# Both halves of head 0's K on one queue, the first weights held until x has landed, K turned ahead of x, and an earlier filler, at the start of a fused attention kernel

## The chip, the cores and the metric

The kernel runs on one core of one Trainium2 chip. The metric is the device time of one execution in microseconds (us). Every version was run several times and is quoted by its median. Ratios are computed as the mean time of one kernel's runs over the mean time of the other's runs of the same rounds, so they are not quite the ratio of the medians quoted beside them. All runs in this study were of the fast state. They were made in batches on different chips (the record numbers four of them 8, 6, 0 and 14), and each batch timed the kernel before as well, so that versions are compared with the before of their own batch.

Two scales meet here. The whole kernel takes 1939 us. The change moves instructions only in its first 16 us, and what it did is about 1.5 us. That is 0.08%, far inside the band of 2% that counts as "same", so the timings carry little on their own, and the argument is read from the traces of the head.

Times inside a trace are us from the start of the profiled span. One trace is one execution, and executions differ: those of the changed kernel in one batch by up to 2.6 us, those of one of the versions below by 4.0 us.

## The reference, cut to what matters

```python
def reference(A_x, A_k_cache, A_v_cache, A_wq, A_wo, B_x, B_w1, B_w3, B_w2):
    xn = _layernorm(x, axis=-1)              # x: 2048 x 640, bf16
    q  = (xn @ wq) -> 32 heads x 2048 x 192
    scores = q k^T * 192 ** -0.5             # k, v: 32 heads x 2048 x 192
    o  = softmax(scores) v
    s  = o @ wo
    g  = silu((silu(xn @ w1) * (xn @ w3)) @ w2)
    return x + s * g
```

## The kernel before

The kernel streams 1024 blocks of scores through TensorE (matmuls), with one exponential of each block on ScalarE. Before the first exponential can run, a head must be worked through: x's first group of 512 rows lands, is normalised, is turned (transposed by TensorE against an identity matrix, then copied by ScalarE or VectorE out of the tile in PSUM that the turns write), and is multiplied by head 0's weights. Head 0's K must be turned and copied as well. K comes in two halves, K0 and K1; each needs 16 turns of 128x128. The weights W come in three parts, all issued by GpSimd.

```python
def load_w0():                       # three loads on GpSimd's queue
    W = wqp.tile([P, 2 * DC, P], BF16, tag="W", name="W")
    nc.gpsimd.dma_start(out=W[:, 0:DC, :], ...)             # first part, 160 KB
    nc.gpsimd.dma_start(out=W[:, DC:2 * DC, 0:PGW], ...)    # second part, 80 KB
    nc.gpsimd.dma_start(out=W[:, DC:2 * DC, PGW:P], ...)    # third part, 80 KB
    ...

def turn_over(k):                    # filler: keeps TensorE busy until data is there
    for i in range(k):
        nc.tensor.matmul(warm, lhsT=ident_bf[:], rhs=ident_bf[:], start=True, stop=True)

def head_start():
    load_x(0, 0, 2)                  # x's first group, SyncE's queue
    load_x(0, 2, 4)
    load_k0(0, nc.sync)              # K0
    load_w0()
    turn_over(44)
    ln_stats(0, 0)                   # statistics of x: three tiles on VectorE, one on ScalarE
    ln_stats(0, 1)
    ln_stats_act(0, 3)
    load_k0(1, nc.scalar)            # K1, ScalarE's queue
    load_x(1, queue=nc.scalar)       # x's second group
    load_v(0, (0,), nc.scalar)       # first half of head 0's V
    ...                              # rest of the statistics; rstd (1/deviation, by pow) on GpSimd
    load_w(1)                        # weights of head 1, GpSimd's queue
    for i in range(4):
        ln_norm(0, i, nc.vector)     # four normalisations on VectorE
    pk0 = ps_o.tile([P, 4, 512], BF16, tag="ob0", name="pk0")
    ln_turn(0, 0, nc.scalar.copy)            # turn x's first half, copy on ScalarE
    turn_k0(pk0, 0, range(4))                # 16 turns of K0
    ln_turn(0, 1, nc.vector.tensor_copy)     # turn x's second half, copy on VectorE
    turn_k0(pk1, 1, (0, 1))                  # 8 turns of K1
    swap_halves(0)
    copy_k0(nc.scalar.copy, pk0, 0, 0)       # copies of K0's turns
    copy_k0(nc.scalar.copy, pk0, 0, 1)
    copy_k0(nc.vector.tensor_copy, pk1, 1, 0)
    load_v(0, (1,))
    load_x(2)
    project_first()                          # 20 matmuls: two x halves, two W halves, 5 each
    turn_k0(pk1, 1, (2, 3))                  # last 8 turns of K1
    copy_k0(nc.scalar.copy, pk1, 1, 1)
    scores(0)
    ...
```

Of the kernel before, what the change touches and what calls it, by code (L numbers as in the profile page):

```python
# [11 lines left out]
BF16 = mybir.dt.bfloat16  # L12
# [3 lines left out]
P = 128  # L16
# [112 lines left out]
def _kernel_impl(  # L129
# [12 lines left out]
    nc = tc.nc  # L142
# [31 lines left out]
    const = ctx.enter_context(tc.tile_pool(name="const", bufs=1))  # L174
# [3 lines left out]
    ident_bf = const.tile([P, P], BF16, name="ident_bf")  # L178
# [25 lines left out]
    ps_o = att.enter_context(tc.tile_pool(name="ps_o", bufs=1, space=bass.MemoryType.PSUM))  # L204
# [4 lines left out]
    x_sb = x_all[:, 0:NQT * D].rearrange("p (t d) -> p t d", d=D)  # L209
# [3 lines left out]
    def load_x(g, t0=0, t1=4, queue=nc.sync):  # L213
        queue.dma_start(out=x_sb[:, 4 * g + t0:4 * g + t1, :],
                          in_=x2[g * 512:(g + 1) * 512, :].rearrange("(p t) d -> p t d", t=4)[:, t0:t1, :])

    def gate_cols(h):
        wsel = B_w1 if h % 2 == 0 else B_w3
        return wsel[:, (h // 2) * PGW:(h // 2 + 1) * PGW]

    def load_w0():
        W = wqp.tile([P, 2 * DC, P], BF16, tag="W", name="W")
        nc.gpsimd.dma_start(out=W[:, 0:DC, :], in_=A_wq[:, 0:P].rearrange("(c p) d -> p c d", p=P))
        nc.gpsimd.dma_start(out=W[:, DC:2 * DC, 0:PGW], in_=gate_cols(0).rearrange("(c p) f -> p c f", p=P))
        nc.gpsimd.dma_start(out=W[:, DC:2 * DC, PGW:P], in_=A_wq[:, P:DH].rearrange("(c p) d -> p c d", p=P))
        loads.setdefault(0, {}).update(W=W)

    def load_w(h):

        W = wqp.tile([P, 2 * DC, P], BF16, tag="W", name="W")  # L230
        nc.gpsimd.dma_start(out=W[0:64, :, :], in_=A_wq[:, h * DH:h * DH + P].rearrange("(j p) d -> p j d", p=64))
        if h < 2 * NPIG:
            nc.gpsimd.dma_start(out=W[64:P, :, 0:PGW], in_=gate_cols(h).rearrange("(j p) f -> p j f", p=64))
        else:
            nc.gpsimd.memset(W[64:P, :, 0:PGW], 0.0)
        nc.gpsimd.dma_start(out=W[64:P, :, PGW:P],
                            in_=A_wq[:, h * DH + P:(h + 1) * DH].rearrange("(j p) d -> p j d", p=64))
        loads.setdefault(h, {}).update(W=W)
# [21 lines left out]
    def load_k0(half, queue):  # L260
        if half == 0:
            kn = stp.tile([P, NQT, HG * DH], BF16, tag="ostage", name="kn")
            k0["v"] = kn[:].rearrange("p t c -> p (t c)")[:, 0:NKT * DH].rearrange("p (j c) -> p j c", c=2 * DH)
            loads.setdefault(0, {}).update(KW=kvp.tile([P, 5, HK], BF16, tag="KW", name="KW"))
        queue.dma_start(out=k0["v"][:, half * HP:(half + 1) * HP, :].rearrange("p j c -> p (j c)"),
                          in_=A_k_cache[0, 0, half * HK:(half + 1) * HK, :].rearrange("(p t) d -> p (t d)", p=P))

    def turn_k0(dst, half, sel):
        for a in sel:
            for b in range(HP):  # L270
                nc.tensor.transpose(out=dst[:, a, b * P:(b + 1) * P],  # L271
                                    in_=k0["v"][:, half * HP + b, FIRST[a]:FIRST[a] + P], identity=ident_bf[:])

    def copy_k0(copy, src, half, two):
        KW = loads[0]["KW"]
        ks = slice(half * HP * P, (half + 1) * HP * P)
        copy(out=KW[:, 0:2, ks] if two == 0 else KW[:, 2:5:2, ks], in_=src[:, 2 * two:2 * two + 2, :])
# [5 lines left out]
    def load_v(h, halves=(0, 1), queue=nc.sync):  # L283


        vt = vts[h % 2]
        for t in halves:
            if h == 0:
                queue.dma_start(out=vt[:, t * NPAIR:(t + 1) * NPAIR, 0:DH],
                                  in_=A_v_cache[0, h, t * HK:(t + 1) * HK, :].rearrange("(i s) d -> i s d", i=P))  # L290
            else:
                nc.sync.dma_start(out=vt[:, :, 0:DH].rearrange("i (p t) d -> i p t d", t=2)[:, :, t, :],
                                  in_=A_v_cache[0, h].rearrange("(p i t) d -> i p t d", i=P, t=2)[:, :, t, :])
        loads.setdefault(h, {}).update(vt=vt)

    mhalf = const.tile([P, 4], F32, name="mhalf")
    nc.vector.memset(mhalf[:], -0.5)
    for vt in vts:
# [9 lines left out]
    def ln_stats(g, i):  # L308
        if i == 0:
            lnorm[g] = [lnp.tile([P, 4, n], F32, tag=t, name=t)  # L310
                        for t, n in (("mv", nc.vector.BN_AGGR_DIM), ("ve", 1), ("rstd", 1))]
        mv, ve, rstd = lnorm[g]
        stats = lnp.tile([P, nsub, nc.vector.BN_STATS_DIM], F32, tag="stats", name="stats")
        xr = x_sb[:, 4 * g + i, :].rearrange("p (a f) -> p a f", a=nsub)
        for a in range(nsub):
            nc.vector.bn_stats(out=stats[:, a, :], in_=xr[:, a, :])  # L316
        nc.vector.bn_aggr(out=mv[:, i, :], in_=stats[:])  # L317
        if i % 2 == 1:
            nc.vector.tensor_scalar(out=ve[:, i - 1:i + 1, 0], in0=mv[:, i - 1:i + 1, 1], scalar1=eps, scalar2=None,
                                    op0=ALU.add)  # L320
            ln_rstd(g, i)

    def ln_rstd(g, i):
        mv, ve, rstd = lnorm[g]
        if i % 2 == 1:
            two = slice(i - 1, i + 1)
            nc.gpsimd.tensor_tensor(out=rstd[:, two, 0], in0=ve[:, two, 0], in1=mhalf[:, two], op=ALU.pow)
# [3 lines left out]
    def ln_stats_act(g, i):  # L331


        mv, ve, rstd = lnorm[g]
        ss = lnp.tile([P, 1], F32, tag="ss", name="ss")
        xns[g, i] = xnp.tile([P, D], BF16, tag="xn", name="xn")
        xi = x_sb[:, 4 * g + i, :]
        nc.scalar.activation(out=xns[g, i][:], in_=xi, func=ACT.Identity, scale=1.0 / D, accum_out=mv[:, i, 0:1])
        nc.scalar.activation(out=xns[g, i][:], in_=xi, func=ACT.Square, scale=-1.0, bias=mv[:, i, 0:1], accum_out=ss[:])
        lnorm["ss"] = ss  # L340
# [222 lines left out]

    pk1 = ps_o.tile([P, 4, 512], BF16, tag="ob1", name="pk1")
    warm = pk1[:, 0, 0:2 * P].bitcast(F32)

    def turn_over(k):
        for i in range(k):
            nc.tensor.matmul(warm, lhsT=ident_bf[:], rhs=ident_bf[:], start=True, stop=True)

    def head_start():

        load_x(0, 0, 2)
        load_x(0, 2, 4)
        load_k0(0, nc.sync)
        load_w0()
        turn_over(44)
        ln_stats(0, 0)
        ln_stats(0, 1)
        ln_stats_act(0, 3)  # L580
        load_k0(1, nc.scalar)
        load_x(1, queue=nc.scalar)
        load_v(0, (0,), nc.scalar)
        ln_stats(0, 2)
        mv, ve, _ = lnorm[0]
        nc.vector.tensor_scalar(out=ve[:, 2, :], in0=mv[:, 2, 1:2], scalar1=eps, scalar2=None, op0=ALU.add)
        nc.vector.tensor_scalar(out=ve[:, 3, :], in0=lnorm["ss"][:], scalar1=1.0 / D, scalar2=eps,
                                op0=ALU.mult, op1=ALU.add)
        ln_rstd(0, 3)
        load_w(1)  # L590
        for i in range(4):
            ln_norm(0, i, nc.vector)
        pk0 = ps_o.tile([P, 4, 512], BF16, tag="ob0", name="pk0")
        ln_turn(0, 0, nc.scalar.copy)
        turn_k0(pk0, 0, range(4))
        ln_turn(0, 1, nc.vector.tensor_copy)
        turn_k0(pk1, 1, (0, 1))
        swap_halves(0)
        copy_k0(nc.scalar.copy, pk0, 0, 0)
        copy_k0(nc.scalar.copy, pk0, 0, 1)  # L600
        copy_k0(nc.vector.tensor_copy, pk1, 1, 0)
        load_v(0, (1,))
        load_x(2)
        project_first()
        turn_k0(pk1, 1, (2, 3))
        copy_k0(nc.scalar.copy, pk1, 1, 1)
        scores(0)
        shift_first()
        shift_k0()
        scores(1)  # L610
        ln_stats(1, 0)
        ln_stats(1, 1)
        ln_stats(1, 2)
        ln_norm(1, 0, nc.vector)
        ln_norm(1, 1, nc.vector)
        ln_turn_dma(1, 0)
        ln_turn_dma(1, 1)
        for g in range(3, NQB):
            load_x(g)
        ln_stats(1, 3)  # L620

    head_start()

    def finish_block(n):
# [71 lines left out]
    for qb in range(NQB):  # L696
        qs = slice(qb * 512, (qb + 1) * 512)
        for fl in range(FL2 // P):
            ps = pools[(qb * (FL2 // P) + fl) % 2].tile([P, 1024], F32, tag="st2", name="ps_gu")
            for r, w in enumerate((wrest["w1"], wrest["w3"])):  # L700
                for c in range(DC):
                    nc.tensor.matmul(ps[:, r * 512:(r + 1) * 512], lhsT=w[:, c, fl * P:(fl + 1) * P], rhs=xnT[:, c, qs],  # L702
                                     start=(c == 0), stop=(c == DC - 1))
# [20 lines left out]
    for i in range(NQT):  # L724
        ps = pools[i % 2].tile([P, 1024], F32, tag="st2", name="ps_f")
        for fc in range(FC):
            for b, (c0, c1) in enumerate(DP):
                nc.tensor.matmul(ps[:, b * 512:b * 512 + c1 - c0], lhsT=hT[:, fc, i * P:(i + 1) * P],  # L728
                                 rhs=w2_sb[:, fc, c0:c1], start=(fc == 0), stop=(fc == FC - 1))
# [78 lines left out]
```

## Time and profile before

| | before |
|---|---|
| time, median of 3 runs | 1939.36 us |
| profiled span | 1936.7 us |
| first half of x's first group landed | 3.86 us |
| third part of W landed (last of its 16 packets' signals) | 8.12 us |
| first projection matmul | 10.44 us |
| first exponential | 14.38 us |

In the views PE is TensorE (PEld its weight loads), DVE is VectorE, ACT ScalarE, POOL GpSimd and SP SyncE; a q behind the name is the engine's sequencer, which issues loads. The page of the kernel before: its span, the busy times, the granted TensorE clock in 40 slices of the span, and the shares of the chain that ended last.

```profile
span 1936.7 us, 59668 instructions
...
PE 1927.1 (100%) x27273; PEld 1317.2 (68%) x27281; DVE 654.4 (34%) x997; ACT 1181.5 (61%) x1278; POOL 282.1 (15%) x501
...
PEclk9999999999999999999999999999999999999999
...
PE 99%; DVE 0%; DMA 0%; ACT 0%; issue 0%
```

TensorE is the bound of the kernel, at full clock, once the head is over. So a change of the head pays only by bringing the first exponential forward, and costs as much as it delays it.

The timeline of TensorE in the head, before. Columns: start, duration, engine, line, operation and tiles, count, and in brackets the idle time ahead of the group with what ended it.

```profile
2.78 4.32 PE L569 MATMUL pk<-ident_bf 128*128 128x128 bf16 x44 [2.78 <-POOL ident_bf masks.py:199]
7.90 0.81 PE L354 MATMUL pst<-ident_bf,xn 128*128 128x128 bf16 x10 [0.80 <-DVE xn L346]
8.54 1.06 PE L271 MATMUL pk<-ident_bf,kn 128*128 128x128 bf16 x16
9.44 0.72 PE L354 MATMUL pst<-ident_bf,xn 128*128 128x128 bf16 x10
10.00 0.61 PE L271 MATMUL pk<-ident_bf,kn 128*128 128x128 bf16 x8
10.44 2.35 PE L391 MATMUL ps<-xnT,W 128*128 128x256 bf16 x20
```

Read it as a queue, since TensorE ran its matmuls in the order of the program: filler (`pk<-ident_bf`), x's first turns (`pst`), K0's turns (`pk<-ident_bf,kn`), x's second turns, half of K1's, and then the projection (`ps`) in one piece. There is almost no idle time from 7.90 on: K's turns sit in the holes that x leaves.

The timeline of ScalarE (ACT), before, same columns: x's copy comes before the two copies of K0.

```profile
8.74 1.23 ACT L356 COPY xnT<-pst 128x1280 bf16<-128x1280 bf16 x1 [2.29 <-PE pst L354]
9.87 1.93 ACT L277 COPY KW<-pk 128x1024 bf16<-128x1024 bf16 x2
...
14.38 2.96 ACT L490 ACTIVATE pT<-st 128x1024 bf16<-128x1024 f32 x3
```

### The profile page before, as it was taken

To read this page: it belongs to the slowest core of one execution; us is meant where nothing else is said; L and a number is where in the kernel's file an instruction comes from. 1 tells how busy PE (TensorE), PEld (TensorE's weight loads), DVE (VectorE), ACT (ScalarE), POOL (GpSimd) and SP (SyncE) were. 2 spreads that over 40 slices of the span, in tenths; PEclk is the share of its full clock that TensorE was granted. 3 is DMA by queue.
4 is the path that set the end of the run, shared out by engine and by line. 5 is a ranking of instruction groups with operands and counts; after the bars stand their busy time and mean duration, and the time that the engine had idled before them with its cause. 6 is when DMAs were issued, how large, how long until landed. Compare 5 with 4: busy or idle time off the path is not lost.

```text
span 1936.7 us, 59668 instructions
## 1 busy us (share of the span) xinstructions
PE 1927.1 (100%) x27273; PEld 1317.2 (68%) x27281; DVE 654.4 (34%) x997; ACT 1181.5 (61%) x1278; POOL 282.1 (15%) x501
## 2 busy tenths in 40 slices
PE   9999999999999999999999999999999999999998
PEld 6666666666666666666666666666666666577776
DVE  7333333333333333333333333333333334521111
ACT  6677676767676767776777777677767677210000
POOL 3111111111111111111111111111111110000000
PEclk9999999999999999999999999999999999999999
DMA  8643433323333434363434343434334220937772
GB/s 181 129 101 67 98 68 85 84 59 92 58 90 61 99 64 97 68 162 68 101 66 100 69 101 69 101 64 100 69 68 97 60 67 2 249 79 137 152 153 60
DMA packets 394643, 178.98 MB, mean 92 GB/s; under 512 B 341616, under 2 KB 382832, under 8 KB 394384
## 3 DMA queue, kind: packets, MB, share of 16 engines
q1 hardware_dynamic: 371136, 125.32, 31.5%
q0 software_dynamic: 19472, 45.71, 10.1%
q8 instruction: 215, 3.52, 0.8%
q10 hardware_dynamic: 3776, 4.06, 0.6%
q14 instruction: 44, 0.36, 0.1%
HBM read 52.82 MB, written 27.79 MB: 42 GB/s over the span
## 4 chain that ended last, share of the span: by engine, by line
PE 99%; DVE 0%; DMA 0%; ACT 0%; issue 0%
PE obank L516 35%; PE st L487 34%; PE ps L424 14%; PE ps_s L111 11%; PE ps_f L728 3%; PE ps_gu L702 1%; PE st L488 1%; PE ps L410 0%; DMA x_all<-in_A_x_dram 0%; DVE stats L316 0%; PE ps L391 0%; PE pst L354 0%; PE pk L271 0%; ACT pT L490 0%; DVE mv L317 0%
## 5 line engine op out<-in xcount | busy, mean ns | idle before, releaser
L490 ACT ACTIVATE pT<-st 128x1024 bf16<-128x1024 f32 x1024 | 1047.4, 1023 | 248.8 <-PE st L488 233.2
L516 PEld LDWEIGHTS <-pT 64*128 64x128 bf16 x16384 | 711.6, 94 | 242.0 <-ACT pT L490 0.2
L516 PE MATMUL obank<-vt,pT 64*128 64x193 bf16 x16384 | 849.6, 243 | 0.0
L487 PE MATMUL st<-qC,KW 64*128 64x512 bf16 x2046 | 605.6, 376 | 0.1
L525 DVE COPY osum<-obank 128x772 f32<-128x772 f32 x128 | 123.1, 962 | 786.9 <-PE obank L516 786.9
L488 PE MATMUL st<-qB,KW 64*128 64x512 bf16 x1024 | 385.0, 376 | 0.0
L487 PE MATMUL st<-qA,KW 64*128 64x512 bf16 x1022 | 384.3, 376 | 0.3 <-ACT pT L490 0.3
L488 PE MATMUL st<-qC,KW 64*128 64x512 bf16 x1022 | 384.3, 376 | 0.0
L488 PE MATMUL st<-qA,KW 64*128 64x512 bf16 x1022 | 384.3, 376 | 0.0
L487 PEld LDWEIGHTS <-KW 64*128 64x128 bf16 x3068 | 278.4, 94 | 153.3 <-issue 2.1
L424 PE MATMUL ps<-xnT,W 64*128 64x512 bf16 x1280 | 297.3, 376 | 0.0
L424 PE MATMUL ps<-xnS,W 64*128 64x512 bf16 x1280 | 296.2, 376 | 0.0
L488 PEld LDWEIGHTS <-KW 64*128 64x128 bf16 x3068 | 278.5, 94 | 0.8 <-issue 0.6
L377 POOL DMA_DIRECT2D qC<-qA x124 | 65.4, 528 | 1283.4 <-DVE rl_all L532 1268.5
L430 ACT CAST qB<-ps 128x512 bf16<-128x512 f32 x131 | 76.8, 586 | 228.2 <-PE ps L424 222.7
L111 PE MATMUL ps_s<-wo_sb,oT 128*128 128x384 bf16 (+3 forms) x1535 | 208.7, 299 | 0.1
L424 PEld LDWEIGHTS <-W 64*128 64x128 bf16 x2560 | 123.6, 94 | 120.7
L111 PEld LDWEIGHTS <-oT 128*128 128x128 bf16 x1536 | 148.4, 98 | 60.4
L526 DVE TENSOR_TENSOR osum<-osum,obank 128x772 f32<-128x772 f32 x128 | 122.7, 959 | 13.4
L533 DVE TENSOR_TENSOR ostage<-osum,rl_all 128x768 bf16<-128x768 f32 x128 | 122.6, 958 | 6.2 <-DMA o_scr<-ostage 1.9
L465 DVE SCALAR_TENSOR_TENSOR hT<-pt,qB 64x512 bf16<-64x512 bf16 x64 | 43.8, 684 | 197.6 <-ACT pt L464 197.6
L429 DVE CAST qA<-ps 128x512 bf16<-128x512 f32 x131 | 90.6, 692 | 25.3 <-PE ps L410 7.2
(84 smaller groups left out, 620.8 us busy)
## 6 DMA issues: line engine op xcount, KB each, us to landing
o_scr<-ostage SPq DMA_DIRECT2D x16, 1536.0 KB, 10.6
vt<-in_A_v_cache_dram SPq DMA_DIRECT2D x63, 384.0 KB, 5.9
qC<-qA POOLq DMA_DIRECT2D x248, 64.0 KB, 2.0
qC<-qB POOLq DMA_DIRECT2D x124, 64.0 KB, 2.3
wo_sb<-in_A_wo_dram POOLq DMA_DIRECT2D x1, 7680.0 KB, 37.8
W<-in_A_wq_dram POOLq DMA_DIRECT2D x32, 160.0 KB, 3.6
W<-in_B_w_dram POOLq DMA_DIRECT2D x32, 80.0 KB, 3.3
W<-in_A_wq_dram POOLq DMA_DIRECT2D x32, 80.0 KB, 2.9
```

The source lines that it names most:

```text
L111: nc.tensor.matmul(ps[:, 0:w], lhsT=oT[:, k, :], rhs=wo_sb[:, k, c0:c1], start=(k == 0), stop=(k == OC - 1))
L377: nc.gpsimd.dma_start(out=qC[0:64, half, :], in_=qAB[half][64:P, :])
L424: nc.tensor.matmul(ps[:, r * 512:(r + 1) * 512], lhsT=W[rows, j, :], rhs=xs[rows, j // 2, qs], start=(j == 0), stop=(j == 2 * DC - 1))
L429: a = nc.vector.tensor_copy(out=qAB[0][:], in_=ps[:, 0:512])
L430: b = nc.scalar.copy(out=qAB[1][:], in_=ps[:, 512:1024])
L487: nc.tensor.matmul(st2[:, 0:512], lhsT=ka, rhs=qa, start=r == 0 and nr == 3, stop=r == nr - 1)
L488: nc.tensor.matmul(st2[:, 512:1024], lhsT=kb, rhs=qb2, start=r == 0 and nr == 3, stop=r == nr - 1)
L490: nc.scalar.activation(out=pT2[:], in_=st2[:], func=ACT.Exp, scale=att_scale)
L516: nc.tensor.matmul(obanks[r][:, j * 256:j * 256 + DH + 1], lhsT=pT2[r * 64:(r + 1) * 64, t * 512 + j * P:t * 512 + (j + 1) * P], rhs=vt[r ...
L525: nc.vector.tensor_copy(out=osum[:], in_=ov[0])
L526: nc.vector.tensor_tensor(out=osum[:], in0=osum[:], in1=ov[1], op=ALU.add)
L533: nc.vector.tensor_tensor(out=ostage[:, qb * 4:qb * 4 + 4, hg * DH:(hg + 1) * DH], in0=osum[:, :, 0:DH], in1=rl.unsqueeze(2).to_broadcast( ...
```

## The change

The intent: have K on the chip early and turn all of it while x is still being normalised, so that nothing of K stands between x's turns and the projection. K1 moves from ScalarE's queue to SyncE's, behind K0. The first weights are held until x has landed (a tiny GpSimd copy reads x and stands ahead of the weights' loads), so that x and K have the transfers to themselves. The filler no longer needs the identity matrix, and so starts at once, 50 matmuls instead of 44.

```diff
+    fill = const.tile([P, P], BF16, name="fill")
+    nc.vector.memset(fill[:], 1.0)
...
+    gate = const.tile([P, 2], BF16, name="gate")
     def turn_over(k):
...
-            nc.tensor.matmul(warm, lhsT=ident_bf[:], rhs=ident_bf[:], start=True, stop=True)
+            nc.tensor.matmul(warm, lhsT=fill[:], rhs=fill[:], start=True, stop=True)
     def head_start():
...
         load_k0(0, nc.sync)
+        load_k0(1, nc.sync)
+        nc.gpsimd.tensor_copy(out=gate[:], in_=x_sb[:, 0, 0:2])
         load_w0()
-        turn_over(44)
+        turn_over(50)
+        pk0 = ps_o.tile([P, 4, 512], BF16, tag="ob0", name="pk0")
+        turn_k0(pk0, 0, range(4))
+        turn_k0(pk1, 1, range(4))
...
-        load_k0(1, nc.scalar)
         load_x(1, queue=nc.scalar)
         load_v(0, (0,), nc.scalar)
+        copy_k0(nc.scalar.copy, pk0, 0, 0)
+        copy_k0(nc.scalar.copy, pk0, 0, 1)
...
-        pk0 = ps_o.tile([P, 4, 512], BF16, tag="ob0", name="pk0")
         ln_turn(0, 0, nc.scalar.copy)
-        turn_k0(pk0, 0, range(4))
         ln_turn(0, 1, nc.vector.tensor_copy)
-        turn_k0(pk1, 1, (0, 1))
         swap_halves(0)
-        copy_k0(nc.scalar.copy, pk0, 0, 0)
-        copy_k0(nc.scalar.copy, pk0, 0, 1)
+        copy_k0(nc.scalar.copy, pk1, 1, 1)
         copy_k0(nc.vector.tensor_copy, pk1, 1, 0)
...
         project_first()
-        turn_k0(pk1, 1, (2, 3))
-        copy_k0(nc.scalar.copy, pk1, 1, 1)
         scores(0)
```

## The prediction

> **What bounds the kernel.** TensorE, busy 1927.1 us of a 1936.7 us span on the page, at full granted clock in all slices, and the chain of waits is 99% PE. The change touches only the head, before the first exponential (14.38 us in the timeline); the order of instructions after the head is the same on every engine in both programs. So the effect is the shift of that exponential, carried to the end: from 15.5 us PE is the limit.
>
> **The chain in the head now** (chain, timeline): x lands 3.86; VectorE statistics and normalisation 3.88 to 9.33; x's turns 7.90 to 8.71 and 9.44 to 10.16, with head 0's K turns in between and after (8.54 to 9.60, 10.00 to 10.61); first projection 10.44 to 12.79 (20 matmuls, 0.11 us each); cast 12.83 to 13.25; scores 13.40; exponential 14.38. The last 8 K turns hide behind that cast.
>
> **What the change does.** (1) All 32 K turns move ahead of x's turns. Only the start of the projection can gain: it waited for PE (ScalarE's copy was done 9.97, weights landed by 8.1). Without K turns x's second turn ends when VectorE's last normalisation (9.33) allows, about 9.8 instead of 10.16. (2) But the built program shows a side effect: the two PSUM buffers are given out in another order. The projection's first tile now takes the buffer that VectorE's copy of x's second half frees, so the first projection matmul waits for both copies; before, for the first copy alone. That copy took 0.82 us: 9.8 + 0.04 + 0.82 = 10.67. The start moves from 10.44 to about 10.7: +0.25 us. (3) ScalarE does two K copies (1.93 us) ahead of x's first copy (1.23 us): K0 lands about 5.5, turns done about 6.8, copies 6.8 to 8.75, x's copy about 8.8 to 10.0. Slack 0.6 us.
> (4) Weights wait for x: issues at about 4.1, 5.0, 5.9 (0.87 to 1.02 us each). Before they took 4.6 to 5.9 us to land; the same gives 9 to 10.5, just in time, a risk. GpSimd's rstd follows at 6.9 instead of 6.3; it had 0.4 us of slack.
> (5) Filler starts at about 1.0 instead of 2.78 us. [...](spacing 107 ns until 6.37 us, 3.6 us after the first, then 56 ns). So [...]filler done 5.6 to 6.0 (nothing on the chain was cold before).
> (6) K's second half, behind the first, lands about 6.5 to 7 instead of 9.0.
>
> **Sum.** 1939.36 + 0.25 (both copies) + 0.05 (share of the risks) = 1939.65 us; range 1938.7 to 1940.8. Chances: faster by over 2% 0.005, within 2% 0.99, slower 0.005.
>
> **What would show it.** Right: first projection matmul near 10.7, released by VectorE's copy of xnT; K turns all before 8; scores near 13.65; first exponential near 14.6; PE busy as before afterwards. Wrong: the projection starts before 10.3; or is released by weights (landing over 10.7) or by ScalarE's copy (K0 landed after 6.5, or filler still cold at 6.3).
>
> **What would make it wrong.** Late weights, +0.3 to +1 us; late rstd; a K half held up by one slow DMA queue (half 0 had one of 16 landings at 7.55, the others by 5.9). The runs before spread over 1 us, more than the effect.

The spacing in (5) is that of the filler's matmuls in the trace of the kernel before: 107 ns from 2.78 us, 56 from 6.37 on. By these figures 50 matmuls from 1.0 us on end at about 5.5, an estimate; the "5.6 to 6.0" lies a little above it.

## The result, and the profile after

| | before | after |
|---|---|---|
| median of 6 runs (lowest to highest) | 1938.84 us (1938.13 to 1939.67) | 1940.24 us (1939.14 to 1941.74) |
| ratio, 95% interval | | 1.0008 [0.9995, 1.0021] |
| profiled span | 1936.7 us | 1938.5 us |
| first projection matmul | 10.44 us | 11.19 us |
| first exponential | 14.38 us | 15.95 us |
| last exponential minus the first | 1628.37 us | 1628.34 us |

The ratio's interval contains 1. The median is 1.4 us higher, and the traces say why: the first exponential is 1.57 us late, and from the first exponential to the last both kernels take the same time to 0.03 us. The rest of the difference of the spans (0.2 us) lies after the last exponential and is not explained here.

The timeline of TensorE in the head, after (columns as before):

```profile
1.07 5.37 PE L572 MATMUL pk<-fill 128*128 128x128 bf16 x50 [1.07 <-DVE fill L297]
6.84 2.22 PE L271 MATMUL pk<-ident_bf,kn 128*128 128x128 bf16 x32 [0.40 <-DMA kn<-in_A_k_cache_dram]
8.90 1.28 PE L356 MATMUL pst<-ident_bf,xn 128*128 128x128 bf16 x20
11.19 0.71 PE L393 MATMUL ps<-xnT,W 128*128 128x256 bf16 x5 [1.01 <-DVE xnT L358]
12.63 1.80 PE L393 MATMUL ps<-xnT,W 128*128 128x256 bf16 x15 [0.74 <-DMA W<-in_A_wq_dram]
14.95 0.39 PE L485 MATMUL st<-qA,KW 128*128 128x512 bf16 x1 [0.52 <-DVE qA L395]
```

All of K's turns are now ahead of x's, as intended. But x's turns start at 8.90 instead of 7.90, although x's first normalised half was ready at the same time as before. Then TensorE idles 1.01 us until x's copies are done, runs 5 matmuls of the projection, and stops: the start-to-start distance from 11.62 to 12.63 is again 1.01 us. Elsewhere in the projection that distance is 0.11 us, so the stop costs 0.90. What ended it is a DMA, the third part of W.

The timeline of ScalarE after:

```profile
7.94 1.93 ACT L277 COPY KW<-pk 128x1024 bf16<-128x1024 bf16 x2 [1.74 <-PE pk L271]
9.76 1.25 ACT L358 COPY xnT<-pst 128x1280 bf16<-128x1280 bf16 x1
```

ScalarE copies K0 first, and x's copy ends at 11.00 instead of 9.97. VectorE's copy of x's other half ends at 11.04, so the projection starts at 11.19.

The chain of waits that ended last, after, in order of time (start, duration, what); before the change it went through VectorE's statistics and normalisation of x:

```profile
3.61 0.18 POOL gate L580
3.79 0.98 POOL W L223
4.77 0.88 POOL W L224
5.64 6.86 DMA W<-in_A_wq_dram
...
12.63 1.81 PE ps L393 x15
```

The longest piece is a transfer of 80 KB that takes 6.86 us from its issue to its landing. Before the change the third part was issued at 3.56 and landed at 8.12, 4.6 us.

The account of this one trace: the projection starts 0.75 us late, the stop costs 0.90, and 0.08 is won back between the end of the projection and the first exponential, where the last 8 turns of K no longer stand. 0.75 + 0.90 - 0.08 = 1.57. (From the start of the projection to the first exponential the kernel before takes 3.94 us; the second trace of the changed kernel, without a stop, takes 3.86.)

### The profile page after: what moved, and what is told of

The parts are those of the page before. It is cut to its first block, busy times and chain, and to the rows that moved or that the text cites. A ratio compares the mean times of both kernels' runs of the same rounds, so it can differ in the third digit from the quotient of the medians.

```text
span 1938.5 us, 59682 instructions
## 1 busy us (share of the span) xinstructions
PE 1928.5 (99%) x27279; PEld 1316.9 (68%) x27287; DVE 654.7 (34%) x998; ACT 1180.2 (61%) x1278; POOL 282.1 (15%) x502
## 4 chain that ended last, share of the span: by engine, by line
PE 99%; DMA 0%; DVE 0%; ACT 0%; POOL 0%; issue 0%; DVEq 0%; ACTq 0%
PE obank L518 35%; PE st L489 34%; PE ps L426 14%; PE ps_s L111 11%; PE ps_f L731 3%; PE ps_gu L705 1%; PE st L490 1%; DMA W<-in_A_wq_dram 0%; PE ps L412 0%; DMA x_all<-in_A_x_dram 0%; ACT pT L492 0%; PE ps L393 0%; POOL W L223 0%; DVE osum L528 0%; POOL W L224 0%
## 6 DMA issues: line engine op xcount, KB each, us to landing
o_scr<-ostage SPq DMA_DIRECT2D x16, 1536.0 KB, 10.5
```

## The experiments

Two questions are open. Why do x's turns and copies come late? And why does the third part of W need 6.86 us? For the second there are three theories:

- A: VectorE's normalisations (7.31 to 9.14 us), which run while the third part is under way (issued at 5.64, landed at 12.50), hold up GpSimd's loads. This was a guess of mine: no trace shows how they would.
- B: GpSimd's own work after the issue, the two pow instructions for rstd (6.54 to 8.16 us), delays the load.
- C: the third part, issued 2.1 us later than before, now shares the transfers with x's second group (640 KB) and V.

The diffs below are shortened: tiles that they declare are left out, and arguments are abbreviated.

In each trace, subtracting the first exponential from that execution's time leaves 1924.1 to 1924.4 us for all versions that leave the rest as it was (1924.7 in one trace, with K's turns back, in which V was late). So "time minus 1924.2" is an estimate of the first exponential of an execution that was only timed.

### Both kernels again

> The kernel before, unchanged, for a second trace and a second set of times. Any theory: ratio 1.000. Wanted are the spreads: x's first landing (3.86 us in the first trace), the projection's first matmul (10.44), its longest inner gap (none), the first exponential (14.38). If these move by more than 0.3 us between two traces of the same program, differences of that size between kernels mean nothing.

> The changed kernel, unchanged, for a second trace. Theory (weights late and turns late): the projection starts near 11.2 us, stops for the third part of the weights, which land near 12.5, and the first exponential comes near 15.95; ratio 1.0007. Rival (the 0.7 us stop was an accident of one execution): weights land before 10.7, exponential near 15.2, ratio 1.0004.

Before again: median 1938.53 us (1938.31 to 1938.78, 4 runs), first exponential 14.42. After again: 1939.85 us (1939.42 to 1940.00, 5 runs), ratio 1.0007 [0.9993, 1.002], first exponential 15.27. Here x's copies were again late (first projection matmul 11.41), but there was no stop:

```profile
11.41 2.34 PE L393 MATMUL ps<-xnT,W 128*128 128x256 bf16 x20 [1.01 <-DVE xnT L358]
```

The third part landed from 10.02 to 11.20 us, just in time. So the loss has a part that repeats, the late projection, and a part that comes and goes, the stop. The second trace has 0.68 us less of a loss than the first; its execution was the fastest of the five, so it may show less than is usual.

### The hold taken away

```diff
-        nc.gpsimd.tensor_copy(out=gate[:], in_=x_sb[:, 0, 0:2])
```

> The changed kernel with the weights no longer held back; all else kept. The build hands the two PSUM buffers out as before again, so the projection's first matmul waits for ScalarE's copy alone. Theory A (two losses, the held weights about 0.75 us and the K turns and K copies ahead of x about 0.75 us): weights land by 8.2, no stop inside the projection, but it still starts at 10.9 to 11.4 because K's second half lands near 8 or later and x's turns and ScalarE's copy of x wait behind K's; first exponential near 15.1; ratio 1.0004. Rival B (only the held weights cost): projection at 10.4 or earlier, exponential at 14.4, ratio 1.000.

Median 1939.75 us (1939.20 to 1940.42, 5 runs), ratio 1.0007 [0.9993, 1.0021]; none of its five runs was below the highest of the nine runs of before (1938.85). All of W had landed at 8.72, and there was no stop; the first projection matmul was at 11.00 and the first exponential at 14.86. The chain of waits of this kernel:

```profile
2.15 5.87 DMA kn<-in_A_k_cache_dram
8.01 0.05 issue
8.06 1.07 PE pk L271 x16
9.13 0.57 PE pst L356 x10
9.70 0.02 issue
9.72 1.23 ACT xnT L358
10.96 0.04 issue
11.00 1.03 PE ps L393 x8
```

This is the other part of the loss, without the stop. K1 lands at 8.01. Its 16 turns stand ahead of x's in TensorE's order, so x's first turns, ready to go at 7.9 in the kernel before, end at 9.70, and everything after them is late. Before the change x's first turns were over at 8.71. The hold is not the whole cause, then, nor even necessary for a loss of about 1 us. It did not bring K early either, which was its purpose: with the hold K1's first packet signals came at 6.38, without it at 7.37, but the last came at 7.95 (8.17 in the second trace) against 8.01.

### The hold alone, put into the kernel before

```diff
         load_k0(0, nc.sync)
+        nc.gpsimd.tensor_copy(out=gate[:], in_=x_sb[:, 0, 0:2])
         load_w0()
```

> The kernel before with only the hold on the first weights added. Theory A: projection starts near 10.4 (K turns as before), its first 5 matmuls run, then it stops for the third part of the weights until about 12.5; first exponential near 15.8, so the hold alone loses about as much as the whole change; ratio 1.0007. Rival B (the third part came late because both halves of K sat on one queue ahead of it): weights land by 10.5, no stop, ratio 1.000.

Median 1940.14 us (1939.82 to 1941.26, 5 runs), ratio 1.0009 [0.9996, 1.0023]; first exponential 16.06. The size was as large as expected, but not by the expected way: there was no stop in the projection. The third part did land late (11.02 to 12.02), yet TensorE was later still. The busy times in two stretches show why (columns: stretch and its length, busy time and count of PE, PE weight loads, VectorE, ScalarE, GpSimd, then granted clock, DMA share, GB/s):

```profile
5.38:8.79 3.41, 1.35 (x23) 1.10 (x21) 3.06 (x11) 0.92 (x2) 3.39 (x5) 1.00 0.83 198
8.79:12.20 3.41, 3.41 (x35) 3.41 (x33) 1.25 (x3) 3.06 (x3) 1.52 (x3) 0.50 1.12 317
```

The clock was granted at half from 8.79 to 12.20. With GpSimd no longer issuing weights first, it built the identity matrix earlier, so the filler ran from 1.38 and was over at 5.90 instead of 7.10. TensorE then idled until 7.96; in the stretch 5.38 to 8.79 it was busy 1.35 us of 3.41; and the next 3.41 us ran at half speed (16 turns of K0 took 1.73 us; 1.06 in the kernel before). The half clock lasted 3.41 us in two other traces as well (8.18 to 11.59 with the queue and the filler alone, 9.81 to 13.22 with only K0 ahead of x, both below) and 6.83 in one (10.56 to 17.39, with the longer normalisations). TensorE was not idle all through the 3.41 us before the fall: it was busy for 1.35 of them. Nor did the full clock come at the same time after the filler's first matmul: 3.6 us in the kernel before (2.78 to 6.36), 5.1 in the changed kernel (1.07 to 6.16). What sets these times is not shown. This was a side effect that none of my theories had.

### K's turns and copies back in their old places, the rest of the change kept

```diff
-        (K0 and K1 turned and copied ahead of x)
+        ln_turn(0, 0, nc.scalar.copy)
+        turn_k0(pk0, 0, range(4))
+        ln_turn(0, 1, nc.vector.tensor_copy)
+        turn_k0(pk1, 1, (0, 1))
+        ... copies, projection, last 8 turns as in the kernel before
```

> The changed kernel with the K turns and K copies put back where they stood (K0 between x's two turns, half of K1 before and half after the projection); the hold on the weights, the early filler of 50 and the one queue for K are kept. Theory A (in-order PE: the turns behind K1's landing cost about 0.6 us of the start): x's turns start at 7.5 to 7.9 again and ScalarE's copy of x ends near 10.0. Then two outcomes, told apart by the clock record: without a fall of the clock the projection starts near 10.4 and stops for the weights' third part until 11.4 to 12.5; with nothing on PE between the filler's end (5.3 to 6.4) and 7.5 the clock may fall to half as it did in the run with the hold alone (8.79 to 12.20 us), then first exponential near 16. Rival B (the hold alone is the loss): same first exponential as the changed kernel, 15.3 to 15.9, always with a stop inside the projection.

Median 1940.52 us (1939.81 to 1942.60, 5 runs), ratio 1.0012 [0.9999, 1.0026]. The timeline of TensorE:

```profile
10.46 0.71 PE L393 MATMUL ps<-xnT,W 128*128 128x256 bf16 x5
11.73 1.80 PE L393 MATMUL ps<-xnT,W 128*128 128x256 bf16 x15 [0.56 <-DMA W<-in_A_wq_dram]
```

The projection starts at 10.46, as in the kernel before (10.44): the late start is the work of K's turns and copies. The stop is there, 0.83 us from 10.90 to 11.73 (a cost of 0.72), with the third part landing from 10.15 to 11.60. So an earlier projection meets the same late weights. In this trace the first half of V also arrived late, which cost another 0.5 us behind the first exponential (15.12). The times did not improve: the median is 2.0 us above the before of its batch, against 1.3 to 1.4 for the whole change, and the traced execution is the fastest of the five. What held the others back is not known; they have no trace.

### Theories A and B for the third part

First, the normalisations in another form, with two tensor inputs, which also takes longer. The expectation was that, if theory A is right, the old form is to blame and the third part comes early; that the new form would not hold up GpSimd's loads was my assumption and was not shown.

```diff
-            engine.tensor_scalar(out=xns, in0=x, scalar1=mean, scalar2=rstd, op0=subtract, op1=mult)
+            engine.scalar_tensor_tensor(out=xns, in0=x, scalar=mean, in1=rstd broadcast, op0=subtract, op1=mult)
```

> The changed kernel; VectorE's four normalisations of the first group are written as an instruction with two tensor inputs (the reciprocal deviation spread over the row) in place of one input and two scalars; same result[...]. Measured is the gap in the weights' queue between its second and third part (8.79 to 9.72 us in the first trace of the change, 8.38 to 8.63 in the second; third part issued 5.64 to 6.51, 3 us before its first packet). Theory A[...]: third part's first packets at about 7.7 to 8, no gap, landed by 10. Theory B (GpSimd's own rstd work after the issues holds it): gap as before, third part from 9.3 or later. Theory C (plain queueing behind K, x and V packets): third part at 9.3 or later as well.

Median 1941.61 us (1940.37 to 1942.89, 4 runs), ratio 1.0013 [0.9998, 1.0029]. The normalisations ran from 7.53 to 10.80 (four in 3.27 us; four in 1.83 in the changed kernel), and the second and third parts landed from 10.08 and from 11.00. The parts came later, not earlier, so what theory A had foretold failed; theories B and C had both said 9.3 or later. The clock also fell to half (10.56 to 17.39), and the first exponential was at 18.52.

Second, more of GpSimd's own work behind the issues:

```diff
         ln_rstd(0, 3)
+        for k in range(2):
+            nc.gpsimd.tensor_tensor(out=more[...], in0=ve[...], in1=mhalf[:, 2:4], op=ALU.pow)
         load_w(1)
```

> The changed kernel with two more GpSimd power instructions (about 0.75 us each, results unused) behind the two it has, ahead of the second head's weights. Theory A[...]: third part's first packets at 9.3 to 10 as in the change. Theory B (GpSimd's own work behind the issues delays them): 1.5 us later, 10.8 to 11.5, and a longer stop of the projection, first exponential 16.5 or later.

Median 1939.27 us (1938.55 to 1942.53, 4 runs), ratio 1.0007 [0.9992, 1.0022]. The third part landed from 10.50 to 11.91, between the changed kernel's two traces (10.89 to 12.50 and 10.02 to 11.20), with 1.4 us more of GpSimd's work behind its issue; theory B had asked for 10.8 to 11.5 for its first packets and a first exponential at 16.5 or later, which came at 15.35. The second part came a little later, from 9.13 to 10.28, and had no one waiting for it. Theory B falls for the third part. The projection stopped for the third part here too (0.87 us, a cost of 0.76). One of its four runs took 1938.55 us, no more than the kernel before: in a lucky execution almost nothing is lost.

Third, no normalisations on VectorE at all: all four on ScalarE, slow on purpose.

```diff
-            ln_norm(0, i, nc.vector)
+            nc.scalar.activation(out=xns[0, i][:], in_=x_sb[:, i, :], func=ACT.Identity,
+                                 scale=rstd[:, i, 0:1], bias=nmr[:, i:i + 1])   # nmr = -mean * rstd
```

> The changed kernel, hold included, with the four normalisations of x's first group on ScalarE instead of VectorE (one tiny VectorE instruction makes their offsets). It will be slow, since ScalarE works longer before its copies; only the weights are to be read. Theory (VectorE's four normalisations, between 7.3 and 9.1 us, keep the third part of the first weights from being issued or written): the third part lands within 1 us of the second, its first packet before 9.7 us. Rival (it is late for another reason, such as GpSimd's own work, or other traffic on the queues): its first packet between 10.0 and 10.9 us as in the two traces of the changed kernel.

Median 1944.68 us (2 runs), slow as announced. The third part landed from 10.48 to 11.58 (the second from 9.27 to 10.57), as late as in the changed kernel, although VectorE did none of the normalisations. Taken like for like (the landings that the expectation's "10.0 to 10.9" was read from), this is the rival's result. Theory A falls as the cause of the late third part. That the normalisations add something, as in the run with the longer ones, is not excluded; that was a single trace.

### Theory C: x's second group and V held until the weights are there

```diff
-        turn_over(50)
+        turn_over(64)
...
+        nc.scalar.copy(out=held[:], in_=W[:, 2 * DC - 1, P - 2:P])   # waits for the third part
         load_x(1, queue=nc.scalar)
         load_v(0, (0,), nc.scalar)
```

This is built on the version with K's turns in their old places.

> The kernel turns_back (hold kept, K's turns and copies in their old places) with two changes that are read apart. First, the load of x's second group and of V's first half, which ScalarE issued at 5.5 to 6.5 us, waits until the third part of the first weights has landed; it is not needed before 14.5 us. Theory C (the third part is late because the packets of x's second group share the saturated queues with it from 7 us on): the third part lands by 9.5 us, against 10.15 to 11.60 in turns_back, the stop of 0.8 us in the projection is gone, and ScalarE is not held beyond 9.6 us. Rival (GpSimd writes the third part late for a reason of its own): it lands at 10 us or later although nothing of x's second group is under way, and ScalarE, which waits for it, copies x only after that. Second, the filler is 64 matmuls long instead of 50. If the pairs of times of turns_back_no_gate (two near 1938.4, three at 1939.6 and more) come from an idle TensorE after a filler that ends early, no stretch at half clock appears in the trace. With both right, first exponential 14.2 to 14.8 and ratio 0.9998 to 1.0004; with either wrong, 1.0006 or more.

The third part landed from 8.17 to 8.86, though it was issued at 5.90 to 6.77, no earlier than in any held version, and VectorE's normalisations (7.57 to 9.39) and GpSimd's work were in their usual places, so that it landed while VectorE was normalising. It had taken until 11.60 in the version it was built on, and until 11.20 to 12.50 in all seven traces with the hold. Theory C is shown, for the two held loads together: x's second group and V's first half were not tried apart. The same stretches from 8.5 to 9.5 us, first in the changed kernel, then here (columns as above; the last two are DMA share and GB/s):

```profile
8.50:9.00 0.50, 0.50 (x13) 0.50 (x10) 0.50 (x2) 0.50 (x2) 0.50 (x2) 1.00 0.96 335
9.00:9.50 0.50, 0.50 (x13) 0.50 (x10) 0.14 (x1) 0.50 (x1) 0.50 (x2) 1.00 0.97 348
```

```profile
8.50:9.00 0.50, 0.50 (x12) 0.50 (x12) 0.50 (x2) 0.12 (x1) 0.50 (x2) 1.00 0.00 0
9.00:9.50 0.50, 0.50 (x13) 0.50 (x11) 0.39 (x2) 0.07 (x1) 0.50 (x1) 1.00 0.00 0
```

In the changed kernel 335 to 348 GB/s are moved at a DMA share of 0.96 to 0.97 while the third part waits (by the trace's packets, 308 KB on ScalarE's queue and 12 KB on GpSimd's from 8 to 9 us); here the last of the weights land by 8.86 and nothing is moved (0 GB/s). How the sharing leaves the third part with so little is not shown; 335 to 348 GB/s is not a ceiling (the kernel before moved 416 from 8 to 9 us). What is shown: two loads on ScalarE's queue delayed one on GpSimd's queue by some 2.7 us (landed by 11.60 with them under way, by 8.86 with them held).

The time did not follow: median 1939.85 us (1939.26 to 1940.38, 5 runs), ratio 1.0007 [0.9993, 1.0021]. The chain of waits says why:

```profile
5.90 2.96 DMA W<-in_A_wq_dram
8.86 0.02 issue
8.88 0.19 ACT held L587
9.07 0.20 ACTq L214
9.27 0.04 issue
9.31 0.62 ACTq L289
9.93 0.04 issue
9.97 1.24 ACT xnT L358
```

The stop in the projection is gone:

```profile
11.34 2.34 PE L393 MATMUL ps<-xnT,W 128*128 128x256 bf16 x20 [0.56 <-ACT xnT L358]
```

But my experiment put its own cost in its place. ScalarE issues the two held loads between 8.89 and 9.93, exactly where it should have copied x; in the version it was built on that copy started at 8.77. I had expected ScalarE to be free by 9.6. First exponential: 15.27. The longer filler, the second change, did as expected: no stretch at half clock in the trace. But the version it was built on had none in its trace either, so this shows little. So it is settled what delays the third part, and whether a better placed version of it recovers the time is not.

### The queue and the early filler alone

Hold removed, and K's turns and copies in their old places: what stays is K1 on SyncE's queue and the filler from 1.07 us.

> The changed kernel without the hold and with the turns and copies of K back in their old places: what stays of the change is both K halves on one queue behind x, and filler from the first microsecond. Theory (the loss is made of the turns of K in front of x's turns, and of the hold; the rest is harmless): first projection matmul 10.4 to 10.6, no stop in the projection, first exponential 14.2 to 14.7, ratio to before 1.000 (within 0.0007). Rival (early filler itself costs, because it ends early, leaves TensorE idle before the first turns and lets its clock fall): the first exponential at 15 or later in the trace, with matmuls at half speed between 8 and 13 us, and a ratio of 1.0008 or more.

Median 1939.60 us against 1938.63 for before, ratio 1.0 [0.9986, 1.0013]. The five times fall apart: 1938.36 and 1938.40, and 1939.60, 1939.63 and 1940.07. The trace is of the slowest. The timeline of TensorE, and its stretches with the granted clock in the third column from the end:

```profile
7.90 1.07 PE L356 MATMUL pst<-ident_bf,xn 128*128 128x128 bf16 x10 [2.12 <-DVE xn L348]
8.76 1.91 PE L271 MATMUL pk<-ident_bf,kn 128*128 128x128 bf16 x16
```

```profile
4.76:8.18 3.42, 1.30 (x23) 1.12 (x20) 3.25 (x13) 1.66 (x4) 1.34 (x2) 1.00 1.02 291
8.18:11.59 3.41, 3.41 (x36) 3.34 (x33) 0.92 (x3) 2.10 (x2) 2.47 (x4) 0.50 1.13 298
```

The filler ended 2.1 us before x was ready, TensorE was busy 1.30 us of the 3.41 from 4.76 on, and the clock fell to half just for the turns: 16 turns of K0 took 1.91 us instead of 1.06. The first exponential came at 15.95, and the projection, which ran at 0.11 us per matmul, started at 12.02. So the rival is right for this execution: with the early filler, and K's loads not on the chain that ended last, 1.57 us were lost. For the two fast runs, which have no trace, it evidently did not cost that. The kernel before has slow executions too: two of its nine in this batch took 1940.30 and 1940.86 us, which is why the ratio of means is 1.0 while the medians differ by 1.0 us. They have no trace, so a part of the split may not belong to this version at all. What decides between the two groups is not shown; I have no trace of a fast one.

I cut the heads of twelve traces (all but before again and the last version below) into stretches of 3.41 us at the clock's own changes. Stretches with 1.29, 1.35 and 1.50 us of TensorE work were followed by the half clock, and stretches at full clock with 2.1 us or more by full clock again; in between, those with 1.65 and 1.87 us were followed by the half clock and those with 1.63, 1.67 and 1.81 were not. In neither of the two traces of the changed kernel did the clock fall, where K's turns from 6.8 or 7.1 us on fill the hole. Whether it fell in some of its other executions (up to 1941.74 us) is open.

### Only K0 ahead of x

Hold removed; K0's turns and copies ahead of x, K1's where they were before the change.

> The changed kernel without the hold, with only the first half of K turned and copied ahead of x; the second half's turns and copies where they were before the change. Theory (the loss without the hold comes from K's second half, which lands near 8 us and whose turns stand in front of x's on the in-order TensorE): x's first turns start at 7.9 to 8.1 instead of 8.96, first projection matmul 9.9 to 10.5, first exponential 13.9 to 14.6, ratio 0.9997 to 1.0003. Rival (the loss without the hold comes from ScalarE, which copies K's first half before x, whichever half is turned when): ScalarE's copy of x starts 9.7 or later, first projection matmul 10.9 or later, first exponential near 14.9, ratio 1.0006 or more.

Median 1940.59 us (1938.73 to 1941.54, 5 runs), ratio 1.0004 [0.9991, 1.0018]. The traced execution cannot decide:

```profile
8.47 1.07 PE L271 MATMUL pk<-ident_bf,kn 128*128 128x128 bf16 x16 [1.91 <-DMA kn<-in_A_k_cache_dram]
```

Here one of K0's 16 packets' signals arrived at 8.42; in most traces the last came between 5.5 and 7.1. Everything of x then stood behind K0 on TensorE, the clock fell after the idle stretch (TensorE busy 1.50 us from 6.40 to 9.81, half clock from 9.81 to 13.22), and the first exponential was at 16.79. Two runs took 1938.73 and 1938.90 us, which by the estimate above means a first exponential near 14.5 to 14.7, where the theory had 13.9 to 14.6 and the rival 14.9. That is a hint, not a proof. What the trace does show is a weakness of the idea itself: with K ahead of x on an engine that works in order, the slowest packet of K holds up x. In the kernel before a packet of K0 that landed at 7.55 us cost nothing, because x's turns came first.

### All of K1's turns behind the projection

Built on the kernel before: 8 turns of K1 moved behind the projection, the other 8 behind the first scores.

```diff
-        turn_k0(pk1, 1, (0, 1))          # ahead of the projection
         project_first()
-        turn_k0(pk1, 1, (2, 3))
+        turn_k0(pk1, 1, (0, 1))
         scores(0)
+        turn_k0(pk2, 1, (2, 3))
         scores(1)
```

> The kernel before with the turns of K's second half moved the other way: none before the projection, half of them after it, half between the first two score rounds (into a PSUM tile of its own, half copies). If TensorE's order is what sets the projection's start (theory A), it starts when ScalarE's copy of x ends, near 10.0 in place of 10.44; first exponential near 14.0 in place of 14.4, ratio 0.9998. Rival B (the start is set by copies and weights): start 10.4, no gain; or the later K turns delay the second scores and nothing is left.

Median 1939.03 us (1938.45 to 1939.67, 5 runs), ratio 1.0003 [0.9989, 1.0017]. The projection started at 9.95 and the first exponential came at 13.88, 0.5 us ahead of the kernel before. The traced executions took 1938.53 us (1938.49 for before), so nothing of it is left at the end. By the eighth exponential the lead is gone, as ScalarE's timeline shows, first of before, then of this version:

```profile
28.25 1.02 ACT L490 ACTIVATE pT<-st 128x1024 bf16<-128x1024 f32 x1 [0.23 <-PE st L488]
```

```profile
28.30 1.02 ACT L491 ACTIVATE pT<-st 128x1024 bf16<-128x1024 f32 x1 [0.23 <-PE st L489]
```

The moved turns take their 0.46 us of TensorE between the first scores, and the copy that went with them makes VectorE start x's second group at 15.32 instead of 14.58. Which of the two takes the lead away was not tested. So there was no version here that beats the kernel before: here the work that left the head came back a few us later, and the lead was gone.

## Why the prediction was right or wrong

The measured median, 1940.24 us, lies in the predicted range and in the predicted class. The centre was too good: it said +0.3 us, and it was +1.4 us against the same rounds of before. (The prediction started from 1939.36 us; with all six runs before is at 1938.84, so a part of the closeness of 1939.65 to 1940.24 is luck, and two of the six runs, 1941.31 and 1941.74, lie above the range.)

- Right: TensorE bounds the rest, and only the shift of the first exponential counts. First to last exponential took 1628.37 and 1628.34 us.
- Right in kind, wrong in size: "the first projection matmul waits for both copies". The profile does name VectorE's copy as what ended that wait. But the start was 11.19, not 10.7. The step that failed is the one on x's turns: "x's second turn ends when VectorE's last normalisation allows, about 9.8". It took K's turns to be over before x needs TensorE ("K turns all before 8"). They ended at 9.06, because K1 landed at 7.95 and not at "6.5 to 7", and x's turns stood behind them. In the version without the hold the chain of waits runs exactly there. With both copies of x late together (ends at 11.00 and 11.04), the exchange of the PSUM buffers cost next to nothing of its own.
- Wrong: "K0 lands about 5.5" and "slack 0.6 us" on ScalarE. The last packet of K0 came at 6.79, the copies of K0 ended at 9.87 and x's copy at 11.00. The slack was used up and more.
- Named as a risk, but mis-sized: the weights. "Before they took 4.6 to 5.9 us to land; the same gives 9 to 10.5, just in time." The third part took 6.86 us and landed at 12.50 (11.20 in the second trace). A duration from issue to landing was carried over to another moment. At the old moment x's second group was not yet under way (its first packets came at 7.67 us in the kernel before); two us later it was (from 7.19 in the changed kernel). Holding that group and V's first half back brought the landing to 8.86. All risks together had been given a share of 0.05 us; this one measured 0.90 in one trace and 0 in the other.
- "Nothing on the chain was cold before", with the filler ending earlier: true for the changed kernel in both traces, though in the first the filler reached full speed at 6.16 and ended at 6.44, not at 5.6 to 6.0. What I missed is what can follow a filler that ends early. In two relatives of the kernel (the hold alone; the queue and the filler alone) TensorE idled 2.1 us behind it, the clock was at half for 3.41 us soon after, and the first exponential of the trace came 1.7 and 1.6 us late.
- The late rstd did not matter: rstd came at 6.54 against 6.30, and the first normalisation at 7.31 against 7.41.

The parts do not add up over the versions. The hold alone cost 1.6 us (median), the late turns without the hold 1.2, the queue and the filler alone 0 or 1 and more, and all together 1.3 to 1.4. With the hold, the queue and the filler but K's turns in their old places it was 2.0, more than for all together. The traces show delays on different engines that hide behind each other, the one that ends last showing; why that version is the slowest of them is open.

Left open: which of these parts the slow executions of the changed kernel (1941.31 and 1941.74 us) had, and whether K1's turns behind x's, with the loads of x's second group placed so that neither the weights nor ScalarE wait, would bring a gain at all. The slow executions of the kernel before (up to 1940.86 us) are unexplained as well.

## What to carry to other kernels

Moving work into an idle stretch of an in-order engine is free only if its data is there before the critical work is ready; judge it by its last packet (here 7.95 and 8.17 us, for an x that was ready at 7.9) and by a bad execution (8.42 for K0 in one), since everything behind it inherits that wait. A time from issue to landing belongs to the moment at which it was measured (80 KB took 4.6 us in the kernel before, 6.86 in the changed one, and 2.96 with the two loads on ScalarE's queue held back): before a load is moved, look at what else will be on the transfers at the new moment. A filler should end just before the work that follows it; starting it earlier without lengthening it moves the idle time to a place where it can hurt (in two traces an idle stretch of 2.1 us there was followed by 3.41 us of half clock, and K0's 16 turns took 1.73 and 1.91 us instead of 1.06).
